# Own places for the queries and keys of heads 2 to 5 in a planned attention and two-layer feed-forward kernel on Trainium2

## The chip, the cores and the metric

The kernel runs on one NeuronCore of one Trainium2 chip. The metric is the device time of one execution in microseconds (us), from the first instruction to the last. The kernel before was timed three times: 1030.91, 1033.85 and 1034.68 us, median 1033.85 us. A core has five engines that run side by side and wait for each other by semaphores: TensorE (PE, with its weight loads in a row of their own, PEld), VectorE (DVE), ScalarE (ACT), GpSimd (POOL) and SyncE (SP). In this kernel SP issues every transfer between main memory and the core, one after the other.

## What is computed

```python
def reference(q, k, v, s, moe_w_a, moe_w_b, moe_w_out, moe2_w_in, moe2_w_out):
    # 4 batches, 8 heads, 576 positions, head size 64; float64 weights, float32 q, k, v, s
    scores = q @ k.T / sqrt(64)
    cum = cumsum(maximum(s, 0))
    scores = where(causal, -1e9, scores + minimum(-(cum[:, None] - cum[None, :]), 0))
    attn = exp(scores - max(scores)); attn /= sum(attn) + 1e-9
    x = (attn @ v) with heads side by side        # 2304 x 512
    x = ((x @ w_a) * (x @ w_b)) @ w_out           # inner width 1536
    r = maximum(x @ w_in, 0); return (r * r) @ w_out2   # inner width 2048
```

## The kernel before, in words

The weights arrive as 64-bit words. "Decoding" turns a block of them into two float32 halves (`wh`, a high part, and `wl`, a low part) with a handful of ACT, DVE and POOL instructions (`split_w`, `decode`, `words`); raw words are fetched into the places `roomxh`, `roomxl` and `words`. Products of the feed-forward layers are three matmuls each (high by high, high by low, low by high).

The first batch's attention is the prologue. `attention(0)` runs over four pairs of heads. For each pair `prep_first` (L531) fetches the values, calls `load_first` (L434) for each head to fetch keys (`fk`) and queries (`fq`) as 64 x 576 tiles, fetches one row of running sums into `fk` as a 65th row, and scales the queries by ACT or DVE (`scaled`). `softmax` then computes scores `st` on PE, row maxima `neg` on DVE and exponentials `e` on ACT; `weigh` transposes (`pt`), copies (`ph`) and multiplies by the values (`av`); `divide` does the division (`rs`). Two banks named `s` hold the first two score pieces of a head, so a head's first piece waits until the exponentials of the head before it have read that bank.

`load_first` takes `fq` from two tiles of the tag `T2q` in turn, and `fk` from the tag `T2k`, which has two buffers. Head 2 therefore waits for head 0, head 3 for head 1, and so on.

The first feed-forward layer of the first 512 positions (`moe1(0)`, "chunk 0", the products `ab` and `py`) follows, with the decoding of its 36 weight blocks and the attention of batch 1 laid between; then come batches 2 and 3, further chunks, and the second layer.

The order of all instructions is made by a planner (`Plan.order`), before anything runs, from costs that are written in the code: each engine takes the operation of lowest rank that can start now by these costs. Where a matmul bank would be taken up after a gap of over 400 ns by the planner's reckoning, the planner puts idle matmuls of the constant tile `warm` before it (`op.idle`), one for each 230 ns of gap; 40 more such matmuls (`glow`, rank `fill`) go wherever PE has nothing else. All of them are called fillers here. They take PE's time and compute nothing.

```python
                gap = t - max(free[e], min(op.bank.tag.free))
                if gap > self.GAP:
                    op.idle = max(op.idle, int(gap / self.BURN))
```

Of the kernel before, what the change touches and what calls it, by code (L numbers as in the profile page):

```python
# [7 lines left out]
F32 = mybir.dt.float32  # L8
# [8 lines left out]
P = 128  # L17
# [246 lines left out]
def attention_moe_moe(tc, q, k, v, s, w_a, w_b, w_out, w_in2, w_out2, out):  # L264
    nc = tc.nc
    B, H, D, S = q.shape
    DM, NT = out.shape
# [9 lines left out]
    GRP = 3  # L277
    GB = 4
# [3 lines left out]
    W = 512  # L282
# [33 lines left out]
    def pool(name):  # L316
        return lambda: pools[name]

    def gated(name, shape, dtype, tag, bufs, nm):
        return pl.tile(pool(name), shape, dtype, tag, bufs, nm, swapped)  # L320

    def sb(shape, dtype, tag, bufs, name):
        return pl.tile(pool("sb"), shape, dtype, tag, bufs, name)

    def at(shape, dtype, tag, bufs, name):
        return gated("at", shape, dtype, tag, bufs, name)
# [38 lines left out]
    def dma(out, in_, kb, takes=(), lag=0.0):  # L365
        pl.call(("SP", kb * 3.0, False, "dma_start", (out, in_), {}), takes=takes, lag=lag)
# [44 lines left out]
    def load_values(b, p):  # L411

        t = at([P, NJ, P], F32, "val", 2, f"val{b}_{p}")
        j = 0
        while j < len(kb):
            k0, m = kb[j]
            j1 = j + 1
            while j1 < len(kb) and kb[j1][1] == m:
                j1 += 1
            dma(  # L420
                t[:m, j:j1].part(j),
                v[b, p, k0 : k0 + m * (j1 - j)].rearrange("(j t) c -> t j c", t=m), m * (j1 - j) * 0.5,
            )
            for i in range(j, j1):
                values[b, p, i] = t[:m, i].part(j)
            j = j1
# [2 lines left out]


    first_q = [at([P, S], F32, "T2q", 2, f"fq{i}") for i in range(2)]
    first_k = {}

    def load_first(hh):  # L434
        tq = first_q[hh % 2]
        tk = first_k[hh] = at([P, S], F32, "T2k", 2, f"fk{hh}")
        dma(tk[:D].part("x"), k[0, hh], S * 0.25)
        dma(tq[:D].part("x"), q[0, hh], S * 0.25)

# [11 lines left out]
    for hh in range(2):  # L451
        load_first(hh)
# [55 lines left out]
    def scaled(n, t):  # L508

        pl.call(  # L510
            on_dve("tensor_scalar", n, t, t, D**-0.5, None, op0=ALU.mult, two=True, each=0.52),
            on_act("mul", n, t, t, D**-0.5),
        )
# [17 lines left out]
    def prep_first(p):  # L531

        load_values(0, p)
        heads = []
        for hh in (2 * p, 2 * p + 1):
            if hh not in first_k:
                load_first(hh)
            tk = first_k[hh]
            dma(tk[D : D + 1].part("c"), cum[hh : hh + 1], 2)
            tq = first_q[hh % 2]  # L540
            scaled(S, tq[:D].part("x"))
            heads.append((tq, tk))
        return heads
# [230 lines left out]
    def attention(b):  # L774
        steps = []

        def unit(p):
            st = {}

            def begin():  # L780
                st["h"] = prep_first(p) if b == 0 else prep(b, p)

            def one(h):
                def f():
                    if h == 0:
                        st["u"] = at([P, S], F32, "u", 2, f"u{b}_{p}")
                        st["one"] = at([P, 2 * len(kb)], F32, "one", 2, f"one{b}_{p}")
                    st[h] = softmax(b, p, h, st["h"][h], st["one"])
                    if h == 1:
                        u = st["u"]  # L790
                        for chunk in weight_banks:
                            weigh(b, p, (st[0], st[1]), chunk, u)
                        divide(b, p, st["one"], u)
                        if b == 0:
                            xh, xl = first_x(p, 0, FIRST)
                            copy(FIRST, xh, u[:, :FIRST])
                            subtract(FIRST, xl, u[:, :FIRST], xh.bitcast(F32))
                            dma(xd[b][0][p].part(p), u[:, FIRST:], (S - FIRST) * 0.5)
                        else:
                            dma(xd[b][0][p].part(p), u, S * 0.5)  # L800

                return f

            steps.extend([begin, one(0), one(1)])
# [789 lines left out]
```

## Time and profile before

| | |
|---|---|
| runs of the kernel before | 1030.91, 1033.85, 1034.68 us |
| profiled execution, span | 1037.2 us (no separate time of this execution is given) |
| PE busy, PEld busy | 1004.5 us (97%), 872.1 us (84%) |
| DVE, ACT, POOL busy | 754.7 (73%), 605.2 (58%), 348.0 us (34%) |
| mean granted TensorE clock | 0.993 of full speed |
| transfers | 243.55 MB, 235 GB/s |

Fillers count as busy PE time. A row of the timeline gives the start, the duration (of several, from the first start to the last end), the engine, the operation with its tiles, and in brackets how long the engine stood idle before it and what ended that. Rows of SPq are issues of transfers; when the data landed is read from the instruction that waited for it.

### The profile page before, as it was taken

To read this page: it belongs to the slowest core of one execution; us is meant where nothing else is said; L and a number is where in the kernel's file an instruction comes from. 1 tells how busy PE (TensorE), PEld (TensorE's weight loads), DVE (VectorE), ACT (ScalarE), POOL (GpSimd) and SP (SyncE) were. 2 spreads that over 40 slices of the span, in tenths; PEclk is the share of its full clock that TensorE was granted. 3 is DMA by queue.
4 is the path that set the end of the run, shared out by engine and by line. 5 is a ranking of instruction groups with operands and counts; after the bars stand their busy time and mean duration, and the time that the engine had idled before them with its cause. 6 is when DMAs were issued, how large, how long until landed. Compare 5 with 4: busy or idle time off the path is not lost.

```text
span 1037.2 us, 16852 instructions
## 1 busy us (share of the span) xinstructions
PE 1004.5 (97%) x5639; PEld 872.1 (84%) x5639; DVE 754.7 (73%) x1557; ACT 605.2 (58%) x1374; POOL 348.0 (34%) x309
## 2 busy tenths in 40 slices
PE   9998989998999999999999999999999999999998
PEld 5667767675778777788889999989999999999998
DVE  5888888767677787346698888688767766876566
ACT  5875768665666665233344454487556665657562
POOL 2233525446444542011122324222325212441123
PEclk9999999999999999999999999999999999999999
DMA  8447687788778786656665767489968866778664
GB/s 218 134 138 217 177 285 209 256 242 259 215 231 239 208 260 210 192 182 228 226 194 177 239 190 262 160 316 366 344 239 330 298 236 253 264 255 296 248 235 162
DMA packets 139254, 243.55 MB, mean 235 GB/s; under 512 B 21272, under 2 KB 91024, under 8 KB 139168
## 3 DMA queue, kind: packets, MB, share of 16 engines
q1 hardware_dynamic: 139168, 242.49, 72.1%
q8 instruction: 44, 0.72, 0.3%
q14 instruction: 42, 0.34, 0.1%
HBM read 181.46 MB, written 52.11 MB: 225 GB/s over the span
## 4 chain that ended last, share of the span: by engine, by line
PE 76%; DMA 12%; DVE 4%; ACT 3%; issue 2%; POOL 1%; SPq 1%; DVEq 0%; POOLq 0%; ACTq 0%
PE ab L261 13%; PE pa L261 9%; PE py L261 8%; PE po_0t L261 6%; PE pw L261 5%; PE pc L261 4%; PE wa L261 4%; PE st L261 4%; PE av L261 3%; PE pt L261 3%; PE wc L261 2%; PE pb L261 2%; PE po_0b L261 2%; PE po_3b L261 2%; PE po_2b L261 2%; PE po_1b L261 2%
## 5 line engine op out<-in xcount | busy, mean ns | idle before, releaser
L261 ACT ACTIVATE e<-st,neg 120x288 f32<-120x288 f32 (+3 forms) x192 | 93.4, 490 | 33.8 <-DVE neg L261 32.1
L261 PE MATMUL py<-g,wh 128*128 128x512 f32 x288 | 93.4, 406 | 1.9 <-DVE y L261 1.5
L261 PE MATMUL ab<-xh,wh 128*128 128x512 f32 x192 | 77.3, 402 | 0.0
L261 PE MATMUL ab<-xh,lo 128*128 128x512 f32 x192 | 75.6, 394 | 0.0
L261 PE MATMUL ab<-xl,wh 128*128 128x512 f32 x192 | 75.5, 393 | 0.0
L261 PE MATMUL pt<-ident,e 120*120 120x120 f32 (+2 forms) x480 | 69.6, 272 | 6.1 <-ACT ph L261 4.8
L261 PEld LDWEIGHTS pt<-ident,e 120*120 120x120 f32 (+2 forms) x480 | 50.5, 134 | 26.9 <-issue 10.1
L261 PEld LDWEIGHTS py<-g,wh 128*128 128x128 f32 x288 | 53.7, 193 | 12.9 <-DVE y L261 1.8
L261 DVE CUSTOM_DVE_ANT_0 st<-st,mask 120x336 f32<-120x336 f32 (+4 forms) x120 | 52.9, 456 | 13.7 <-PE st L261 12.3
L261 PE MATMUL ab<-x,wh 128*128 128x512 f32 x192 | 62.1, 405 | 0.0
L261 PE MATMUL av<-ph,val 120*64 120x240 f32 (+3 forms) x512 | 58.7, 360 | 0.0
L261 PE MATMUL py<-g,loo 128*128 128x512 f32 x144 | 57.5, 399 | 0.0
L261 DVE COPY ph<-pt 120x360 f32<-120x360 f32 (+3 forms) x82 | 42.1, 529 | 17.5 <-PE pt L261 16.3
L261 PE MATMUL st<-T 66*120 66x336 f32 (+1 forms) x144 | 44.8, 324 | 8.9 <-ACT e L261 7.6
L261 PEld LDWEIGHTS av<-ph,val 120*64 120x64 f32 (+1 forms) x512 | 31.3, 136 | 22.6 <-issue 10.5
L261 ACT COPY ph<-pt 120x360 f32<-120x360 f32 (+3 forms) x78 | 34.0, 446 | 18.0 <-PE pt L261 17.4
L261 DVE TENSOR_TENSOR ab<-ab,a 128x512 f32<-128x512 f32 x36 | 25.2, 699 | 24.8 <-PE ab L261 23.3
L261 PEld LDWEIGHTS ab<-xh,lo 128*128 128x128 f32 x192 | 36.5, 190 | 8.0
L261 PEld LDWEIGHTS ab<-xh,wh 128*128 128x128 f32 x192 | 36.4, 190 | 7.1
L261 PEld LDWEIGHTS ab<-xl,wh 128*128 128x128 f32 x192 | 36.5, 190 | 6.9
L261 ACT CAST g<-ab 128x512 fp32r<-128x512 f32 x36 | 21.1, 585 | 35.8 <-DVE ab L261 35.7
L261 PEld LDWEIGHTS ab<-x,wh 128*128 128x128 f32 x192 | 35.5, 191 | 7.5
(693 smaller groups left out, 3166.6 us busy)
## 6 DMA issues: line engine op xcount, KB each, us to landing
w<-w2q SPq DMA_DIRECT2D x48, 896.0 KB
lo<-wlab SPq DMA_DIRECT2D x36, 512.0 KB
w2q<-w2ip SPq DMA_DIRECT2D x48, 256.0 KB
w2s<-w2op SPq DMA_DIRECT2D x48, 256.0 KB
loo<-wlo SPq DMA_DIRECT2D x24, 384.0 KB
w2ir<-in_moe_w_in SPq DMA_DIRECT2D x16, 512.0 KB
w2or<-in_moe_w_out SPq DMA_DIRECT2D x16, 512.0 KB
ws_0t<-w2s SPq DMA_DIRECT2D x12, 512.0 KB
```

Of the source, the lines that this page charges most:

```text
L261: getattr(eng, method)(*map(real, args), **{k: real(a) for k, a in kw.items()})
```

## The change

Head 2 and 3 get tiles of the tag `g` (four buffers), heads 4 and 5 tiles of `loo` for the queries and `lo` for the keys; these tags serve the feed-forward layers later. Heads 6 and 7 take the two old query tiles again. Every query tile gets its row of ones from POOL at the start, six where there were two. Nothing else is edited.

```diff
     first_q = [at([P, S], F32, "T2q", 2, f"fq{i}") for i in range(2)]
+    first_q += [sb([P, 2 * W], F32, "g", GB, f"fq{i}")[:, :S] for i in (2, 3)]
+    first_q += [sb([P, 2 * GRP * P], F32, "loo", 2, f"fq{i}")[:, :S] for i in (4, 5)]
+    AHEAD_HEADS = len(first_q)
     first_k = {}
 
     def load_first(hh):
-        tq = first_q[hh % 2]
-        tk = first_k[hh] = at([P, S], F32, "T2k", 2, f"fk{hh}")
+        tq = first_q[hh % AHEAD_HEADS]
+        if hh in (2, 3):
+            tk = sb([P, 2 * W], F32, "g", GB, f"fk{hh}")[:, :S]
+        elif hh in (4, 5):
+            tk = sb([P, 2 * DM], F32, "lo", 3, f"fk{hh}")[:, :S]
+        else:
+            tk = at([P, S], F32, "T2k", 2, f"fk{hh}")
+        first_k[hh] = tk
         dma(tk[:D].part("x"), k[0, hh], S * 0.25)
         dma(tq[:D].part("x"), q[0, hh], S * 0.25)
@@ prep_first
-            tq = first_q[hh % 2]
+            tq = first_q[hh % AHEAD_HEADS]
```

Since a planner sets the order, the edit moves instructions on all engines. Three places follow.

SP, the transfers after the first values, before: `fk_213` is head 2's key, `roomxh`, `roomxl` and `words` take the first weights.

```order
L261 DMA val_1_120<-in_v 120x4x128
L261 DMA cd<-cl 32x576
L261 DMA roomxh<-in_moe_w_a 128x4x256
L261 DMA roomxh<-in_moe_w_b 128x4x256
L261 DMA roomxl<-in_moe_w_out 128x1024
L261 DMA words_199<-in_moe_w_a 128x4x256
L261 DMA fk_213<-in_k 64x576
L261 DMA fq_87<-in_q 64x576
```

And in the changed program (`fk_143`, `fq_131` are head 2's, `fk_164`, `fq_141` head 3's).

```order
L261 DMA val_1_120<-in_v 120x4x128
L261 DMA fk_143<-in_k 64x576
L261 DMA fq_131<-in_q 64x576
L261 DMA fk_143<-cum 1x16x36
L261 DMA fk_164<-in_k 64x576
L261 DMA fq_141<-in_q 64x576
L261 DMA fk_164<-cum 1x16x36
L261 DMA fk_176<-in_k 64x576
```

Nine more transfers follow before the first weights do: the rest of heads 4 and 5 with the second half of `cd` among them, and head 6's three, which wait for head 0's tiles. The first weight transfer stands 15 places later than before.

ACT, from the scaling of head 0's queries to head 0's exponentials, before:

```order
L261 ACTIVATE fq_87<-fq_87 64x576
L261 CAST ch<-cum 32x576
L261 ACTIVATE fq_102<-fq_102 64x576
L261 ACTIVATE e_0_0_188,sum_133<-st_0_0_0_155,neg_131 120x336
L261 ACTIVATE e_0_0_188,sum_133<-st_0_0_0_155,neg_131 96x96
```

And changed:

```order
L261 ACTIVATE fq_87<-fq_87 64x576
L261 CAST ch<-cum 32x576
L261 ACTIVATE fq_102<-fq_102 64x576
L261 ACTIVATE fq_131<-fq_131 64x576
L261 ACTIVATE fq_141<-fq_141 64x576
L261 ACTIVATE e_0_0_208,sum_192<-st_0_0_0_145,neg_188 120x336
L261 ACTIVATE e_0_0_208,sum_192<-st_0_0_0_145,neg_188 96x96
```

The scaling of heads 2 and 3 now stands ahead of head 0's first exponential. Heads 4 to 7 are scaled by DVE.

PE, from head 0's last score piece to head 1's first, before:

```order
L261 MATMUL st_0_0_3_196<-fk_79,fq_87 120x456
L261 LDWEIGHTS plain
L261 MATMUL st_0_0_3_196<-mask,plain 120x120
L261 MATMUL st_0_1_0_204<-fk_93,fq_102 120x336
L261 LDWEIGHTS plain
L261 MATMUL st_0_1_0_204<-mask,plain 120x120
```

And changed:

```order
L261 MATMUL st_0_0_3_170<-fk_79,fq_87 120x456
L261 LDWEIGHTS plain
L261 MATMUL st_0_0_3_170<-mask,plain 120x120
L261 LDWEIGHTS warm
L261 MATMUL glow<-warm 128x512
```

The last two rows stand there eleven times, and head 1's first piece follows them. Counted over the whole program, PE has 5248 matmuls of the computation in both, and 87 fillers before, 97 after. Before, 13 fillers stand between head 1's pieces and head 2's first piece, with 13 transposes (`pt`) of heads 0 and 1 among them; after, 11 stand before head 1, 1 within it and 7 before head 2, and the 13 transposes come later. From there to the first product of chunk 0 there are 21 before and 20 after. In chunk 0 there are none before, and 9 and 2 after (at a `pt` of batch 1's first pair and at a `py` of the second group). Up to the start of chunk 2 the change has 6 fewer (5 at a `py`, 1 at chunk 2's first product). From chunk 2 on no filler is left, and the two programs run almost in the same order.

## Rows read from the trace of the kernel before

**Rows 1.** The page, busy time by engine (microseconds, share of the span, instructions).

```profile
PE 1004.5 (97%) x5639; PEld 872.1 (84%) x5639; DVE 754.7 (73%) x1557; ACT 605.2 (58%) x1374; POOL 348.0 (34%) x309
```

**Rows 2.** Windows: stretch, length, busy time by engine, granted clock, DMA share, GB/s.

```profile
20.00:40.00 20.00, 18.93 (x125) 12.57 (x123) 15.32 (x44) 14.66 (x39) 7.63 (x6) 1.00 0.65 176
40.00:60.00 20.00, 20.00 (x151) 14.10 (x149) 16.03 (x46) 15.04 (x49) 5.12 (x4) 1.00 0.38 113
60.00:80.00 20.00, 19.39 (x126) 11.99 (x124) 16.81 (x36) 14.88 (x35) 6.42 (x5) 1.00 0.51 152
...
500.00:1040.00 540.00, 524.24 (x2950) 507.38 (x2948) 397.81 (x695) 300.29 (x602) 159.63 (x140) 1.00 0.72 252
```

**Rows 3.** Timeline of PE, from head 1's first score piece to head 2's.

```profile
13.04 0.78 PE L261 MATMUL st<-fk,fq 65*120 65x336 f32 x2
...
16.62 0.81 PE L261 MATMUL glow<-warm 128*128 128x512 bf16 x3
...
17.27 0.76 PE L261 MATMUL pt<-ident,e 96*96 96x96 f32 x6
...
17.87 1.03 PE L261 MATMUL glow<-warm 128*128 128x512 bf16 x4
...
18.87 1.07 PE L261 MATMUL pt<-ident,e 120*120 120x120 f32 x7
...
19.78 1.46 PE L256 MATMUL st<-warm 128*128 128x512 bf16 x6
...
22.22 0.83 PE L261 MATMUL st<-fk,fq 65*120 65x336 f32 x2 [0.98 <-DVE fq L261]
```

**Rows 4.** Timeline of SP's issues and of what waited for queries, first 22 us.

```profile
3.07 0.60 SPq L261 DMA_DIRECT2D fq<-in_q  x1
...
6.25 0.69 ACT L261 ACTIVATE fq<-fq 64x576 f32<-64x576 f32 x1 [0.21 <-DMA fq<-in_q]
...
7.82 0.44 SPq L261 DMA_DIRECT2D cd<-cl  x1
...
8.30 0.42 SPq L261 DMA_DIRECT2D roomxh<-in_moe_w_a  x1
...
13.73 0.60 SPq L261 DMA_DIRECT2D fq<-in_q  x1
...
14.37 0.59 SPq L261 DMA_DIRECT2D fk<-cum  x1
15.01 0.58 SPq L261 DMA_DIRECT2D words<-in_moe_w_b  x1
...
21.71 0.45 DVE L261 TENSOR_SCALAR fq<-fq 64x576 f32<-64x576 f32 x1 [2.46 <-DMA fq<-in_q]
```

**Rows 5.** Timeline of ACT and DVE, head 0's maxima and exponentials.

```profile
10.88 0.67 DVE L261 TENSOR_REDUCE neg<-st 120x1 f32<-120x336 f32 x2 [4.06 <-PE st L261]
...
11.67 0.54 ACT L261 ACTIVATE e<-st,neg 120x336 f32<-120x336 f32 x1 [4.74 <-DVE neg L261]
...
12.66 0.44 ACT L261 ACTIVATE e<-st,neg 120x216 f32<-120x216 f32 x1
```

**Rows 6.** Timeline of PE, its stalls of over 1 us in chunk 0.

```profile
103.41 0.47 PE L261 MATMUL st<-T 66*120 66x456 f32 x1 [2.02 <-ACT e L261]
...
141.39 0.39 PE L261 MATMUL st<-T 66*120 66x288 f32 x1 [2.68 <-ACT e L261]
...
187.22 0.98 PE L261 MATMUL pt<-ident,e 120*120 120x120 f32 x4 [1.45 <-ACT ph L261]
```

**Rows 7.** Windows of 4 us around the second of these, columns as in rows 2.

```profile
140.00:144.00 4.00, 2.61 (x10) 2.21 (x11) 3.59 (x9) 2.88 (x9) 0.95 (x1) 0.87 0.67 173
144.00:148.00 4.00, 4.00 (x17) 3.20 (x17) 1.81 (x4) 1.37 (x4) 0.00 (x0) 0.70 1.00 341
```

**Rows 8.** Timeline, chunk 0's first product and the start of the stages after it.

```profile
76.14 0.58 PE L261 MATMUL ab<-x,wh 128*128 128x512 f32 x1
...
85.63 0.57 ACT L261 CAST g<-ab 128x512 fp32r<-128x512 f32 x1
...
90.11 0.55 SPq L261 DMA_DIRECT2D loo<-wlo  x1
```

## The prediction, made before the changed kernel ran

> **What bounds the kernel now.** I read the page first, then windows over the whole span, then the timeline of PE with its stalls, then the timelines of SP and ACT in the first 25 us. The page [rows 1] says that PE is busy 97% of the span, and the windows [rows 2] say the same of nearly every stretch: the first batch's attention has a full 20.00 us between 40 and 60 us, 18.93 between 20 and 40, and 19.39 between 60 and 80. Part of this is filler, so the timeline has to be looked at as well [rows 3]. Head 1's scores start at 13.04 us and are done at 16.62; head 2's start at 22.22. Between them lie 13 transposes and 13 fillers, and a stall of 0.98 us that the scaling of head 2's queries ended. Why that scaling is late, SP and DVE show [rows 4]: the queries were asked for at 13.73 us, behind four weight transfers, and DVE could start on them at 21.71, 7.98 us later. Queries asked for at 3.07 us, with little else in flight, were in use at 6.25, after 3.18 us. So the change goes at a real wait. The question is what it is worth once the fillers and the order of the other engines have moved too.
>
> Behind the prologue the stalls of PE are few: in chunk 0 there are three of 2.02, 2.68 and 1.45 us, all ended by ACT [rows 6]. After the second the granted clock is 0.87 and 0.70 in two stretches of 4 us [rows 7], a mix of PE's two levels, 2.4 and 1.2 GHz; that is 4 x 0.13 + 4 x 0.30 = 1.7 us on top of the stall.
>
> **The prologue, step by step.** Head 0's scores end at 13.04 us in both programs, for all that stands ahead of them on SP is the same, and the four extra memsets on POOL come after the two that head 0 needs; the memsets that they delay (of the maxima's tiles) would be in use at 10.88 us [rows 5], long after.
>
> *PE.* A filler costs (17.27 - 16.62) / 3 = 0.217 us [rows 3]. Now 11 of them come first, 2.39 us. Head 1's pieces, with the three transposes among them, take 16.62 - 13.04 = 3.58 us as before; one filler among them and seven behind are 1.74 us. Head 2 then starts at 13.04 + 2.39 + 3.58 + 1.74 = 20.75 us, 1.47 us sooner. But the 13 transposes that stood before it are still to do, and cost 17.87 - 17.27 = 0.60 and 19.78 - 18.87 = 0.91, or 1.51 us [rows 3]. With them PE is at 22.26 us where it was at 22.22: **0.0 us**. The wait of 0.98 us goes, and six more fillers, 1.30 us, take its place.
>
> *ACT.* The scaling of heads 2 and 3 now stands ahead of head 0's first exponential, which started at 11.67 us [rows 5]. SP issued `cd` at 7.82 us, where head 2's key will now be, and issues one transfer each 0.64 us (13.73, 14.37, 15.01) [rows 4]. Head 3's queries are four places behind: 7.82 + 4 x 0.64 = 10.38 us. With the 3.18 us of the quiet row they land at 13.56; after the scaling of 0.69 us [rows 4] the first exponential starts at 14.25, 2.6 us late. Behind it on ACT is all of head 0; who waits is PE, for the bank of head 1's first piece. That bank is free 12.66 - 11.67 = 0.99 us after the first exponential starts [rows 5], at 15.24. PE's eleven fillers end at 13.04 + 2.39 = 15.43. So the delay is just covered, with 0.2 us to spare, and I cost it at nothing. At the far end, with the 7.98 us of the loaded row, the queries land at 18.36, and PE waits 4.6 us. I take the quiet row, since the weights that shared the queue in the other now come after; the traffic is only the heads' own.
>
> The Trainium skill speaks against the change at this place: "TensorE: Matmul & The Clock Gate", Part 2, on each phase, says that PE is the only engine that reorders, so exponentials that could run stand still behind a scaling that waits for its data. By that rule the late landing gives the slower rival below; were ACT free to pass, there would be no such case. No row here shows it either way.
>
> *The rest of the prologue.* From 22 to 76 us PE has one filler less, -0.2 us, and otherwise the same matmuls; the stalls that are left there are 0.61 us between 60 and 80 us [rows 2]. The gain here can't be above about 0.8 us: the fillers are in the program and PE has to run them.
>
> *The weights.* Their first transfer stands 15 places later, 8.30 + 15 x 0.64 = 17.9 us [rows 4]. The first product starts at 76.14 us [rows 8], which covers it; what is lost is the head start for the blocks after. At that product the changed program has decoded 5 high parts where it had 8, and fetched 11 blocks where it had 12; at the second group of `py` it is level again (22 to 20 high parts). Cost 0 if ACT and DVE catch up in their idle time, else the slower rival. The other moved transfer, `cd`, is read in batch 1 alone, after 76 us.
>
> *The borrowed tiles.* Head 5's scores are done by 60 us, the first new use of `g` is at 85.63 us and of `loo` at 90.11 [rows 8]. So nothing waits for them: 0.
>
> **Chunk 0 and after.** There the changed program has 11 fillers that were not there, 11 x 0.217 = +2.4 us, and up to chunk 2 six fewer, -1.3 us. Both are bounded by zero: where PE would stall anyway, a filler costs nothing, and where a stall is left bare, a missing filler saves nothing. I count both in full: +1.1 us, between -1.3 and +2.4. From chunk 2 on the order is nearly the same, and PE is busy 524.24 of the 537 us that are left from 500 us on [rows 2]; 0.
>
> **Sum.** 0.0 - 0.2 + 1.1 = **+0.9 us**, with bounds of -2.3 and +2.4 before the rivals. The profiled execution spans 1037.2 us, so it would become 1038.1; that execution is 3.35 us above the median of the three runs, 1033.85, and the same sum on the median is **1034.8 us**. A measurement can tell about 0.5% from no change, 5.2 us.
>
> **The rivals.** *Slower, head 3's queries land late.* One place: ACT's fifth ACTIVATE. If the queries take longer than 3.18 + 0.2 us, PE waits for each further microsecond. At the loaded row's 7.98 us it is 4.6 us, and a clock that falls as at 141 us adds 1.7: +6.3, or 1041 us. For: three transfers of values and one of sums are still in flight just before. Against: no weights are. Chance 0.12.
>
> *Slower, the decoding stays behind.* Three high parts less at 76 us mean that ACT, which ended all three stalls of chunk 0, has more to do in it. Two further stalls like the one at 141 us with their clock, 2 x (2.68 + 1.7) = 8.8, of which the 11 fillers cover 2.4: +0.9 + 6.4, or 1041 us. It decides from the point where a product of chunk 0's third or fourth step waits for `wh`. Chance 0.16.
>
> *Faster, stalls of chunk 0 go.* The new order shifts ACT's work against PE's there. If the stalls at 141 and 187 us vanish with their clock, that is 2.68 + 1.45 + 2 x 1.7 = 7.5 us: 1034.8 - 7.5 = 1027 us. For: all the stalls hang on ACT's order, which is new. Against: nothing in the change relieves ACT. Chance 0.17.
>
> *Faster, PE is not the bound of the prologue.* If matmuls and fillers only looked busy, DVE with 15.32 and 16.03 us in the 40 us from 20 to 60 [rows 2] would set the pace, and earlier queries could take up to 40 - 31.35 = 8.7 us off: 1026 us. Against it stands that the matmuls there follow each other without a stall. The Trainium skill's "Perfetto Trace Analysis", Identifying the Most-Contended Engine, holds for it: matmul busy time is a poor measure and weight loads are the better one; by the loads, 12.57 and 14.10 us, PE had room. Chance 0.05.
>
> *The fetches don't come early.* The order shows that they do, so only 0.02, and the time is then as before.
>
> **How the numbers follow.** The forecast has 0.48; its own range is 1031 to 1038, the bounds with the spread of the runs. With the rival that changes nothing, "same" is 0.50. Faster is 0.17 + 0.05 = 0.22, slower 0.12 + 0.16 = 0.28. The range takes in the slower rivals at 1041 and the larger faster one at 1027, and reaches from 1026 to 1042 us; what it leaves out is stalls in greater number on either side.
>
> **What would show it.** Right: head 0's first exponential near 14.2 us with DMA as its releaser, head 2's first piece near 20.8 with no wait for `fq`, the first `ab` within 1 us of 76.14. Wrong: PE waiting between the eleven fillers and head 1; stalls in chunk 0 ended by `wh` or by a weight transfer; the first `ab` more than 2 us earlier; or a difference that first arises after 400 us.

## The result, and the profile after

The changed kernel took 1042.2 us (median of 12 runs, 1039.33 to 1050.82), the kernel before 1034.09 us (12 runs, 1030.53 to 1039.33): a ratio of 1.0087, 95% interval 1.0065 to 1.0109. It is slower by 0.9%, or 8.1 us, where the forecast was no change.

The page's busy times and three windows answer to [rows 1, 2].

```profile
PE 1008.8 (97%) x5640; PEld 873.3 (84%) x5649; DVE 752.0 (72%) x1559; ACT 610.1 (58%) x1385; POOL 329.4 (32%) x300
```

```profile
20.00:40.00 20.00, 19.55 (x142) 13.65 (x142) 15.44 (x45) 14.02 (x46) 3.79 (x3) 1.00 0.73 225
...
60.00:80.00 20.00, 19.82 (x128) 13.25 (x127) 16.05 (x37) 14.75 (x35) 5.07 (x4) 1.00 0.62 179
...
500.00:1040.00 540.00, 527.37 (x2949) 508.18 (x2947) 399.08 (x695) 302.67 (x607) 153.84 (x141) 1.00 0.72 250
```

PE is as busy as before, and even in the prologue a little busier. The prologue itself answers to [rows 3 to 5]. The timelines of SP, ACT and PE in it, and of chunk 0's first product [rows 8]:

```profile
10.24 0.59 SPq L261 DMA_DIRECT2D fq<-in_q  x1
...
17.75 0.58 SPq L261 DMA_DIRECT2D roomxh<-in_moe_w_a  x1
...
13.29 0.68 ACT L261 ACTIVATE fq<-fq 64x576 f32<-64x576 f32 x1 [0.54 <-DMA fq<-in_q]
13.88 0.52 ACT L261 ACTIVATE e<-st,neg 120x336 f32<-120x336 f32 x1
...
12.92 2.54 PE L261 MATMUL glow<-warm 128*128 128x512 bf16 x10
15.29 0.73 PE L261 MATMUL st<-fk,fq 65*120 65x336 f32 x2
...
20.55 0.73 PE L261 MATMUL st<-fk,fq 65*120 65x336 f32 x2
...
74.77 0.81 PE L261 MATMUL ab<-x,wh 128*128 128x512 f32 x2
```

Head 3's queries, asked for at 10.24 us, let the first exponential start at 13.88; head 1 follows the fillers at 15.29 without a wait, head 2 starts at 20.55 (22.22 before) and chunk 0 at 74.77 (76.14 before). The weights are first asked for at 17.75 us, 9.45 us later than before. Of chunk 0, [rows 6] is not the whole: in the kernel before it lasts until chunk 1's first product at 258.80 us, and three more stalls of PE in it are over 1 us, one of 1.26 us at 180.64 us, ended by ACT, and two ended by a transfer:

```profile
235.19 0.38 PE L261 MATMUL st<-T 66*120 66x336 f32 x1 [1.24 <-DMA t2k<-kh]
...
236.92 0.38 PE L261 MATMUL st<-t2k,t2q 128*120 128x336 f32 x1 [1.34 <-DMA t2k<-kh]
```

The three longest after, up to chunk 1's first product at 257.36 us, were all ended by ACT. The longest two are 1.84 us each, in place of 2.68 and 2.02:

```profile
116.97 0.40 PE L261 MATMUL st<-T 66*120 66x288 f32 x1 [1.30 <-ACT e L261]
...
138.69 0.47 PE L261 MATMUL st<-T 66*120 66x456 f32 x1 [1.84 <-ACT e L261]
...
255.37 0.54 PE L261 MATMUL st<-T 66*120 66x216 f32 x1 [1.84 <-ACT e L261]
```

Up to chunk 2 these two executions show no loss. Chunk 2's first product, before and after:

```profile
433.83 0.58 PE L261 MATMUL ab<-xh,wh 128*128 128x512 f32 x1
```

```profile
433.60 0.58 PE L261 MATMUL ab<-xh,wh 128*128 128x512 f32 x1
```

At 533 us they are still level. There the last group of chunk 2's `py` runs beside the first products of the stage that takes the remaining 768 positions in two halves of 384 (tiles `wa`, `wb`, `wc`, `pw`; called the wide stage below). PE before:

```profile
533.09 0.73 PE L261 MATMUL py<-g,wh 128*128 128x512 f32 x2 [1.47 <-DVE y L261]
...
542.56 0.33 PE L261 MATMUL wb<-b21hx,wh 128*128 128x384 f32 x1
...
667.60 0.33 PE L261 MATMUL pa<-b11h,w 128*128 128x384 f32 x1
```

and after:

```profile
533.07 0.73 PE L261 MATMUL py<-g,wh 128*128 128x512 f32 x2 [0.70 <-DVE y L261]
...
545.10 0.44 PE L261 MATMUL wb<-b21hx,wh 128*128 128x384 f32 x1 [2.40 <-DVE y L261]
...
672.56 0.34 PE L261 MATMUL pa<-b11h,w 128*128 128x384 f32 x1
```

From level at 533 us the changed kernel falls 4.96 us behind by the second layer's first product (`pa`). 2.40 us of that is one stall, which the addition `y` on DVE ended. DVE and the transfer it waits for, before:

```profile
536.85 0.55 SPq L261 DMA_DIRECT2D lo<-wlab  x1
...
538.72 1.22 DVE L261 TENSOR_TENSOR wx<-ws,wx 128x1024 fp32r<-128x1024 f32 x1
539.87 0.68 DVE L261 TENSOR_TENSOR y<-py,y 128x512 f32<-128x512 f32 x1
...
543.59 1.28 DVE L261 TENSOR_TENSOR ws<-wh,lo 128x512 f32<-128x512 f32 x2
544.79 0.68 DVE L261 TENSOR_TENSOR y<-py,y 128x512 f32<-128x512 f32 x1
```

and after:

```profile
536.77 0.55 SPq L261 DMA_DIRECT2D lo<-wlab  x1
...
538.71 1.23 DVE L261 TENSOR_TENSOR wx<-ws,wx 128x1024 fp32r<-128x1024 f32 x1
542.23 2.21 DVE L261 TENSOR_TENSOR ws<-wh,lo 128x512 f32<-128x512 f32 x2 [2.30 <-DMA lo<-wlab]
544.37 1.28 DVE L261 TENSOR_TENSOR y<-py,y 128x512 f32<-128x512 f32 x2
```

DVE is free at the same moment in both, and `lo` was asked for at the same moment. Before, DVE adds the first `y` ahead of the sums `ws`, and when it comes to these at 543.59 us, nothing has to be waited for. After, both `ws` stand ahead of both `y`: DVE waits 2.30 us for `lo`, `y` waits behind, and with `y` the bank that `wb` needs. Then the granted clock falls. The windows from 540 us, before and after (columns as in [rows 2], the clock third from the end):

```profile
540.00:544.00 4.00, 4.00 (x22) 3.63 (x21) 3.97 (x6) 0.89 (x2) 1.40 (x1) 1.00 0.91 323
544.00:548.00 4.00, 4.00 (x23) 3.78 (x23) 3.79 (x9) 0.79 (x2) 0.00 (x0) 1.00 0.84 271
```

```profile
540.00:544.00 4.00, 2.70 (x14) 2.10 (x12) 1.77 (x2) 0.61 (x2) 3.29 (x3) 1.00 1.01 309
544.00:548.00 4.00, 2.90 (x10) 2.90 (x11) 3.28 (x8) 0.69 (x1) 0.00 (x0) 0.69 0.85 292
548.00:552.00 4.00, 4.00 (x20) 3.61 (x19) 1.80 (x6) 1.03 (x2) 0.00 (x0) 0.88 0.69 205
```

At 0.69 and 0.88 of 2.4 GHz, a mix with 1.2 GHz, 4 x 0.31 + 4 x 0.12 = 1.7 us go. With the stall that is 4.1 of the 4.96 us; for the rest no single row was found. Another 1.5 us are lost between there and the end (spans 1037.2 and 1043.7 us), which is no more than profiled executions differ by: over the 18 of this case that last stretch takes 366.6 to 373.1 us. No instruction named here reads the first batch's queries.

### The profile page after: what moved, and what is told of

Its sections match the earlier page's. It is cut to its first block, busy times and chain, and to the rows that moved or that the text cites. A ratio compares the mean times of both kernels' runs of the same rounds, so it can differ in the third digit from the quotient of the medians.

```text
span 1043.7 us, 16850 instructions
## 1 busy us (share of the span) xinstructions
PE 1008.8 (97%) x5640; PEld 873.3 (84%) x5649; DVE 752.0 (72%) x1559; ACT 610.1 (58%) x1385; POOL 329.4 (32%) x300
## 4 chain that ended last, share of the span: by engine, by line
PE 59%; DMA 4%; DVE 3%; ACT 1%; issue 1%; SPq 0%; DVEq 0%; POOL 0%; ACTq 0%
PE ab L261 9%; PE pa L261 8%; PE po_0t L261 6%; PE py L261 5%; PE pw L261 4%; PE pc L261 4%; PE wa L261 4%; PE wc L261 2%; PE pb L261 2%; PE po_3b L261 2%; PE po_1b L261 2%; PE po_0b L261 2%; PE po_2b L261 2%; PE po_3t L261 1%; PE po_1t L261 1%; PE av L261 1%
## 5 line engine op out<-in xcount | busy, mean ns | idle before, releaser
L261 PE MATMUL py<-g,wh 128*128 128x512 f32 x288 | 90.8, 396 | 1.3 <-DVE y L261 0.7
L261 ACT COPY ph<-pt 120x360 f32<-120x360 f32 (+3 forms) x87 | 38.2, 450 | 30.7 <-PE pt L261 29.9
L261 DVE COPY ph<-pt 120x360 f32<-120x360 f32 (+3 forms) x73 | 37.6, 524 | 12.1 <-PE pt L261 11.8
L261 PE MATMUL st<-t2k,t2q 128*120 128x336 f32 (+1 forms) x144 | 40.2, 303 | 0.4 <-DMA t2k<-T 0.2
```

The lines of the kernel that those rows point to most:

```text
L261: getattr(eng, method)(*map(real, args), **{k: real(a) for k, a in kw.items()})
```

## The experiments

Each ratio is to the kernel before on the same chip, with its 95% interval. The kernel before measured 1033.5 to 1034.87 us beside them.

**Head or tail: e1 and e2.** The order up to chunk 2's first product comes from one kernel, the rest from the other.

```diff
+OWN, TAIL, CUT = True, False, (2, 0, 0)   # e1; e2: False, True
...
+        at = next(i for i, op in enumerate(mine) if op.key == self.cut)
+        head, rest = mine[:at], {op.key: op for op in mine[at:]}
+        for key, eng, idle in tail:
+            if key in rest:
+                op = rest.pop(key)
+                op.eng, op.idle = eng, idle
+                head.append(op)
+        return head
```

> The changed kernel up to the first product of chunk 2; from there on the order of the kernel before. Theory A (the loss is made by the new order of the last chunk before the second layer, where DVE's wait for `lo` stands ahead of the additions `y`): the changed prologue and chunks 0 and 1 cost nothing (in the two traces chunk 2's first product starts at 433.8 and 433.6 us), so the ratio to the kernel before is 1.000, between 0.997 and 1.003, and the 2.40 us stall of PE behind `y` is gone. Theory B (the loss belongs to the early fetch and its new tiles, wherever it shows): the ratio stays at 1.009, above 1.005.

> The mirror: the kernel before with its own tiles and order up to the first product of chunk 2, from there on the order that the changed kernel has. Theory A: the loss is here, a ratio of 1.005 to 1.009, with a PE stall of about 2.4 us before the second `wb` of the last chunk and a clock window of about 0.8 behind it. Theory B: no loss, 0.997 to 1.003.

Measured: e1 1037.65 us, 1.0027 [1.0007, 1.0047]; e2 1041.13 us, 1.0048 [1.0025, 1.0072]. Both ends cost, the tail too, which the edit does not touch; the two intervals overlap, so which costs more does not follow from these. e2 has the stall before `wb` (2.23 us), e1 has not.

**The two additions: e3 and e4.** The changed kernel with `ws` moved behind `y` on DVE, and the kernel before with `ws` moved ahead.

```diff
+    ws = [order[place["ws", i]] for i in range(2)]
+    if MOVE == "y first":        # e3
+        to = max(place["y", 2], place["y", 3])
+        keep = [op for op in order if op not in ws]
+        n = keep.index(order[to]) + 1
+    else:                        # e4
+        n = min(place["y", 2], place["y", 3])
+        keep = [op for op in order if op not in ws]
+        n = keep.index(order[n])
+    order = keep[:n] + ws + keep[n:]
```

> The changed kernel, with one move on DVE: the two additions `ws` of the last chunk's fourth block, which wait for `lo`, stand behind the two additions `y` instead of ahead of them. Theory A: the 2.40 us stall and the clock loss of 1.7 us behind it go, so the time falls by about 4 us, to a ratio of about 1.005 to the kernel before; the rest of the loss, which arises later in the same chunk, stays. Rival (the stall only moves to the next wait on DVE): under 1.5 us better, a ratio above 1.007.

> The kernel before, with the opposite move: the two additions `ws` stand ahead of the two additions `y`. Theory A: DVE waits for `lo` until about 542 us, PE stalls some 2.4 us behind it and loses 1.7 us of clock, so the ratio is about 1.003 to 1.004. Rival (in the old order `lo` has landed in time, or the stall is caught up later): within 1.001.

Measured: e3 1038.26 us, 1.0029 [1.0012, 1.0046]; e4 1039.99 us, 1.0052 [1.0033, 1.007]. Two instructions of DVE take 0.58% off the changed kernel (1.0087 to 1.0029), and the same two put 0.52% on the kernel before. In e3 DVE's `y` waits only for PE, `ws` for nothing, and `wb` starts without a stall:

```profile
541.25 0.69 DVE L281 TENSOR_TENSOR y<-py,y 128x512 f32<-128x512 f32 x1 [1.14 <-PE py L281]
541.86 2.18 DVE L281 TENSOR_TENSOR ws<-wh,lo 128x512 f32<-128x512 f32 x2
...
542.12 0.33 PE L281 MATMUL wb<-b21hx,wh 128*128 128x384 f32 x1
```

In e4 the wait and the stall are there, in a kernel that is otherwise the one before:

```profile
538.03 1.29 DVE L281 TENSOR_TENSOR ws<-wh,lo 128x512 f32<-128x512 f32 x2 [2.28 <-DMA lo<-wlab]
...
539.98 0.44 PE L281 MATMUL wb<-b21hx,wh 128*128 128x384 f32 x1 [1.47 <-DVE y L281]
```

Two things say that these two additions are all of the tail's loss that can be told from the noise. e3, with the new tail and `y` first, measured the same as e1 with the old tail (1.0029 and 1.0027). And from chunk 2's first product to the first `pa`, the four profiled executions with `ws` ahead of `y` and a stall at `wb` (after, e2, e4, n2) take 238.96, 236.90, 238.65 and 238.51 us, the other 14 all 233.5 to 234.3.

**Chunk 0's fillers: e5.** e1 without the 9 and 2 fillers of chunk 0.

```diff
+    for op in order:
+        if op.key < pl.cut if op.key is not None else False:
+            op.idle = 0 if op.idle in (2, 9) else op.idle
```

> The kernel of the first experiment (changed kernel up to chunk 2, old order from there, ratio 1.0027) without the 9 and 2 fillers that the changed order has in chunk 0. Theory A (these fillers are the rest of the loss): 11 x 0.217 = 2.4 us come back, a ratio of 1.000 to 1.001, with PE going on to the same products without a stall. Rival (PE waits there anyway, for ACT or DVE, and loses clock on top): the ratio stays at 1.002 to 1.005.

Measured: 1039.08 us, 1.0049 [1.0025, 1.0073], not below e1. The fillers are not what the head loses by. In the stretch from 125 to 150 us PE is busy 19.41 us, in e1 22.72: idle time has taken their place.

**The tiles without the order: e6 and e7.** e6 has the new tiles, and on every engine, SP's fetches among them, the order of the kernel before. e7 is e6 without the 13 fillers ahead of head 2.

```diff
+        for key, eng, idle in tail:
+            op = rest.pop(key)
+            op.eng, op.idle = eng, idle
+            head.append(op)
...
+    glows = [op for op in order if op.rank[0] == 4][18:25]   # e7
+    order = [op for op in order if op not in glows]
+    [op for op in order if op.idle][2].idle = 0
```

> One part of the change alone: heads 2 to 5 have their own tiles, but every engine keeps the order of the kernel before. SP no longer waits for head 0's tiles, so head 2's fetch goes out right behind the fourth weight transfer, near 10.4 instead of 13.2 us, and lands behind 2 MB of weights. Theory A (what costs is the new order, not the tiles): the 0.98 us stall before head 2 shrinks or goes, nothing else changes, a ratio of 0.998 to 1.001. Rival (tiles in other places or earlier traffic cost by themselves): above 1.002.

> The last one, and the 13 fillers between head 1's scores and head 2's are left out, 2.8 us of PE. If the fillers held PE back once the queries are early, head 2 starts up to 2.8 us sooner than there and chunk 0's first product with it: a ratio of 0.996 to 0.999. If PE waits for the fetch, the exponentials or the copies there anyway, the idle time takes their place: 0.999 to 1.002, or more where the granted clock falls behind the idle time.

Measured: e6 1034.84 us, 1.0000 [0.9977, 1.0023]; e7 1035.55 us, 1.0013 [0.9988, 1.0039]. The tiles cost nothing. Of e7 the section on the hardware says more.

**The same without the edit: n2.** The kernel before with one constant of the planner changed by one, and nothing else. **n2y** is n2 with `ws` moved as in e3.

```diff
-    LATE = {"PE": 120.0, "DVE": 90.0, "ACT": 120.0, "POOL": 120.0, "SP": 2000.0, "CTL": 0.0}
+    LATE = {"PE": 120.0, "DVE": 90.0, "ACT": 121.0, "POOL": 120.0, "SP": 2000.0, "CTL": 0.0}
```

> The kernel before with one number of the planner changed, ACT's delay of 120.0 ns to 121.0, an edit that does nothing on the chip but gives another order. Theory C (the size of the loss is that of any new order, not of the early fetch): the time moves by 0.3 to 1% too, most likely up. Rival (a new order alone costs nothing, the loss needs the early fetch): within 0.2% of the kernel before.

> The kernel before with one planner constant changed by one (ACT's delay 121 for 120, no tile and no fetch changed), which alone took 1042.95 us, and with the two ws additions put behind the two y additions on DVE. If the place of these two additions is the greater part of what a re-planned order costs here too, 1036 to 1039 us, without the stall of 2.2 us before the wide stage's third wb product and without the half clock behind it. If the re-planned order loses elsewhere, 1042 to 1043 us still.

Measured: n2 1042.95 us, 1.0082 [1.0045, 1.0119]; n2y 1039.52 us, 1.0054 [1.0032, 1.0076]. A re-planned order costs as much as the change did, with no tile and no fetch changed. n2 has the same two rows:

```profile
538.64 2.68 DVE L261 TENSOR_TENSOR ws<-wh,lo 128x512 f32<-128x512 f32 x2 [1.66 <-DMA lo<-wlab]
...
541.98 0.47 PE L261 MATMUL wb<-b21hx,wh 128*128 128x384 f32 x1 [2.23 <-DVE y L261]
```

In n2y they are gone, and `wb` starts at 536.14 us with no stall. Its time is just above what was expected, and the two intervals overlap, so the times alone don't show what the additions cost n2. n2y is clear of the kernel before all the same: something else is left, and no run shows what.

**Where in the head: e8, e9, e11, e12.** As e1, with the cut at chunk 0's first product (e8), chunk 1's (e9), head 2's first score (e11) and head 4's (e12).

```diff
-OWN, TAIL, CUT = True, False, (2, 0, 0)
+OWN, TAIL, CUT = True, False, (0, 0, 0)   # e8; e9: (1, 0, 0)
...
+            if (b, hh, i) == CUT:             # e11: (0, 2, 0); e12: (0, 4, 0)
+                pl.cut = pl.key
             pe(cost, calls, ps, ins)
```

> The changed kernel's order up to chunk 0's first product, and from there the order of the kernel before. The kernel that kept the new order up to chunk 2 lost 0.27% (1037.65 us) and its trace stood some 4 to 5 us behind at batch 1's scores in chunk 0. Theory A, the new order inside chunks 0 and 1 is what costs it: this one is within 0.1% of the kernel before, 1034 to 1035.5 us. Theory B, what the prologue hands over (fewer decoded weights, transposes left for later) costs it: 1037 to 1038 us again, with the delay in the old order's waits at the start of chunk 0.

> The changed kernel's order through chunk 0, the old order from chunk 1's first product on. If chunk 0 (or the prologue) is the place, 1037 to 1038 us as with the cut at chunk 2; if chunk 1 is the place, 1034 to 1035.5 us, as the kernel before.

> The changed kernel's order on every engine up to head 2's first score piece (the eleven fillers, the early scaling and fetches in it), the old order of all that is left from there. If these first 21 us cost it, 1037 to 1040 us as with the whole new prologue; if what follows in the prologue does, 1034 to 1035.5 us.

> The same cut at head 4's first score piece, in the middle of the prologue. Together with the cuts at head 2 and at chunk 0 it brackets the place: 1034 to 1035.5 us if the second half of the new prologue costs the 0.3 to 0.6%, 1037 to 1040 us if the first half does.

Measured: e8 1039.65 us, 1.0050 [1.0025, 1.0075]; e9 1039.97 us, 1.0059 [1.0038, 1.008]; e11 1043.31 us, 1.0095 [1.0071, 1.012]; e12 1046.5 us, 1.0125 [1.0098, 1.0152]. e9 costs no less than e1, so the new order of chunk 1 is not needed for the head's loss. The other three do not place it further, for each stops PE near its own join, where the old order takes over from the new. In e8 that is at the start of chunk 0, where ACT waits for a weight:

```profile
87.21 0.67 ACT L280 ACTIVATE roomxl<-roomxl 128x512 f32<-128x512 f32 x1 [2.53 <-DMA roomxl<-in_moe_w_out]
...
90.82 1.22 PE L280 MATMUL ab<-x,wh 128*128 128x512 f32 x2 [3.63 <-DVE g L280]
```

Between 74 and 100 us the changed kernel, e1, e3, e5 and e9 have no stall above 0.2 us. e11 stops for 3.65 us at 24.23 us and e12 for 3.80 at 39.84, both behind a copy `ph` on DVE. So e8 does not show that the prologue's new order costs anything where chunk 0's new order follows it.

**The edit without the planner: e10.** Own tiles, and on SP alone the new order up to chunk 0. The other engines keep theirs.

```diff
+NEW = ('SP',)
...
+        order = {}
+        for e in self.LATE:
+            order[e] = [x for x in (by_new if e in NEW else by_old) if x[1] == e]
```

> The own tiles and, on SP alone, the changed kernel's order up to chunk 0: the queries and keys of heads 2 to 5 are asked for early and the first weights 15 places later, while PE, ACT, DVE and POOL keep every instruction, filler and place of the kernel before. This is the edit without what the planner made of it. If the fetch is a gain by itself, the stall of 1 us before head 2 goes and the time is 1033 to 1034 us. If the late weights are what the new prologue costs (its order alone measured 1037.65 to 1039.97 us in four kernels), 1038 to 1040 us, with waits for wh or for a weight transfer in the prologue or chunk 0. If it is the order of the other engines' work, within 0.15% of the kernel before.

Measured: 1048.46 us, 1.0155 [1.0127, 1.0183], the slowest of all, and beyond each of the three expectations. The timelines of DVE and PE, and the window, show why:

```profile
21.76 0.43 DVE L328 TENSOR_SCALAR roomxh<-roomxh 128x512 f32<-128x512 f32 x1 [6.51 <-DMA roomxh<-in_moe_w_a]
...
23.66 1.23 PE L328 MATMUL pt<-ident,e 120*96 120x120 f32 x5 [6.20 <-ACT e L328]
...
20.00:40.00 20.00, 16.34 (x104) 11.03 (x105) 13.75 (x40) 12.40 (x35) 5.09 (x4) 0.83 0.55 171
```

The first decoding step stands on DVE amid the row maxima of head 1. It waits 6.51 us for weights that were asked for at 17.76 us; behind it wait the maxima, the exponentials and PE, and the clock of 0.83 costs another 20 x 0.17 = 3.4 us. Together 9.6 us, of which 6.5 are left at chunk 0's first product (82.67 us, 76.14 before); by chunk 2's it is 9.6 again (443.42 and 433.83).

**The edit with the weights in place: e13 and e14.** The old order on every engine, own tiles. e13 pulls the transfers of heads 2 to 5 forward only behind the first four weights; e14 pulls head 2's alone ahead of them.

```diff
+EARLY, ANCHOR = (2, 3, 4, 5), 2   # e13; e14: (2,), "cl"
...
+        keys = [k for hh in EARLY for k in self.marks[hh]]
...
+        early = [by[k] for k in keys]
...
+        head = keep[:at] + early + keep[at:]
```

> The old order on every engine, own tiles, and on SP the transfers of heads 2 to 5 pulled forward only to the place that head 2's have in the kernel before, behind the first four weights. Theory, the lateness of the first weights is the whole price of the early fetch in e10 (1048.46 us, with DVE standing 6.5 us at a decoding step): with those weights in place it is gone, 1033.5 to 1036 us. Rival, the early fetch costs by its traffic or by the places that it takes on SP from the weights behind: 1038 us or more, with waits for words or for raw queries.

> The old order on every engine, own tiles, and only head 2's three transfers ahead of the first weights, which come 3 x 0.64 = 1.9 us later. In e10 the first weight landed 4.0 us after its issue; here that is at about 8.3 + 1.9 + 4.0 = 14.2 us, and the decoding step on DVE starts at 15.5, so it should not wait. Head 2's queries are there early, and a stall of up to 1 us before head 2 goes: 1033 to 1035 us. If weights later by 2 us cost already, 1037 us or more.

Measured: e13 1036.32 us, 1.0022 [1.0003, 1.0042]; e14 1034.46 us, 1.0003 [0.9982, 1.0025]. With the weights in place nearly all of e10's loss is gone. e10 has other transfers of SP in new places too, but with the 6.51 us in its trace the weights' lateness is its main cause. In e14 the decoding step runs when DVE reaches it:

```profile
15.61 0.41 DVE L292 TENSOR_SCALAR roomxh<-roomxh 128x512 f32<-128x512 f32 x1
```

e14 has head 2's queries early and no wait for them, and gains nothing that its interval could show. In e13 all twelve transfers share the stretch behind the weights, and head 2's queries are as late as in [rows 4]:

```profile
21.90 0.45 DVE L292 TENSOR_SCALAR fq<-fq 64x576 f32<-64x576 f32 x1 [3.09 <-DMA fq<-in_q]
```

No version was faster than the kernel before.

## Why the prediction was wrong, point by point

**What bounds the kernel: right, but only for the stretch that was read.** The wait for head 2's queries was real in that execution, but it is not there each time: e2 and e4 have the prologue of the kernel before, and in their profiled executions head 2 starts at 21.47 and 21.35 us without a wait, with the queries as late as before. In e2:

```profile
20.27 0.45 DVE L280 TENSOR_SCALAR fq<-fq 64x576 f32<-64x576 f32 x1 [0.62 <-DMA fq<-in_q]
...
21.47 0.73 PE L280 MATMUL st<-fk,fq 65*120 65x336 f32 x2
```

The fillers ahead of head 2 cover it there. e14, with the queries early, starts head 2 at 21.45 and stays at 1.0003 [0.9982, 1.0025]; a gain of 0.98 us, 0.1%, would be too small for these runs to tell.

**The prologue: right.** The first exponential was put at 14.25 us and came at 13.88, with a DMA as the releaser of the scaling ahead of it; head 1 at 15.43 and 15.29; head 2 at 20.75 and 20.55; chunk 0's start within 1 us of 76.14, and it was 74.77, 1.4 us earlier; most of that is the stall of the one execution, for e2 and e4 start chunk 0 at 75.28 and 75.16. The quiet row was the right choice for the landing. The borrowed tiles at 0 were right (e6, 1.0000).

**Chunk 0's fillers, +1.1 us: not borne out.** e5 has eleven fillers fewer than e1 and is not faster. By its trace they stood in time that PE would have idled away, which the step had as its bound of zero.

**"From chunk 2 on the order is nearly the same ...; 0": this is the step that failed.** It took nearly the same for the same. Two additions out of some 1,500 instructions on DVE had moved ahead of a third, the first `y`, and in e3 and e4 that is worth 0.58% and 0.52%, or 5 to 6 us: the stall, and in most of the traces the clock behind it. The text even named "a difference that first arises after 400 us" among what would show it wrong, but gave it no price and no chance. The order could have been read there: an instruction that waits for a transfer had come to stand ahead of one that PE waits for. The Trainium skill's "TensorE: Matmul & The Clock Gate", Part 2, on each phase, which the prediction used for ACT, says that only PE reorders; it holds for DVE in this trace, where `y` stands behind `ws` for the 2.30 us. It was applied to the one engine and place that the edit touched.

**The weights, "Cost 0 if ACT and DVE catch up", and the rest of the head: 0.3 to 0.6% in place of nothing.** e1, e5 and e9, all with the new order through chunk 0 and the old tail, measured 1.0027, 1.0049 and 1.0059. The rival "the decoding stays behind" had about this price in total (1041 us) but another place: no stall of over 1 us in chunk 0 was ended by `wh`; that the measured 1042.2 us lies next to it is luck. What is shown: the loss comes with the new order of prologue and chunk 0 (e9), not with the tiles (e6) nor with chunk 0's fillers (e5); the early fetch by itself costs 1.55% through late weights (e10), and 0.2% or nothing where the weights stay in place (e13, e14). That the planner, which moved the decoding back to suit late weights, turned those 1.55% into 0.3 to 0.6% is a reading that fits these and is not shown; which wait carries it in the changed kernel is open. The two profiled executions could not show it, since they are level at 433 us. The one of before was a late one there: of four executions with the old prologue (before, e2, e4, e6) chunk 2's first product starts at 433.83, 429.70, 429.77 and 430.97 us, mean 431.1; of six with the new (after, e1, e3, e5, e8, e9) at 433.60, 435.16, 434.16, 435.73, 431.27 and 435.24, mean 434.2. That is 3.1 us, or 0.3%, between means whose ranges overlap. The planner's other order, n2 and n2y, is not late there (431.33 and 428.10), so not every new order brings this loss.

**The sum.** Instead of +0.9 us: some 3 from the head (e1, e3 and the 3.1 us above) and 5 to 6 from the wide stage, against 8.1 measured.

**The other rivals.** Head 3's queries landed in time (13.29 us). The prediction's three stalls of chunk 0, "all ended by ACT", were six over 1 us, two of them ended by a transfer. The longest became shorter (1.84 us in place of 2.68), and it did not show: chunk 0 takes 182.7 us to chunk 1's first product before and 182.6 after. That PE is not the bound of the prologue found no support: with the queries early, no part of the 8.7 us came off that shows (e14).

## What to carry to other kernels

Where a planner sets the order, an edit's smallest part may be the edit: n2, with one cost changed by one, lost about as much as this change. So the difference of the two orders is to be read to the end on every engine, above all for an instruction that waits for a transfer and has moved ahead of one on which PE depends; and the edit is tested by holding the order fixed (e6, e14), or a re-planned order is taken for the cause. A fetch that is pulled forward delays those it passes: ask what stands behind the first use of each.

## What the runs showed of the hardware that was not expected

A short stall can cost twice, but need not. The 2.40 us before `wb` were followed by 1.7 us of lower clock, while the kernel before passes the same place at 1.00. n2's 2.23 us came with 0.78 and 0.79 in the two windows from 540 us. In e2 the same stall, as long as in n2 and ending at 540.74 us, left the clock at 1.00:

```profile
540.00:544.00 4.00, 3.26 (x18) 3.13 (x19) 3.91 (x10) 0.69 (x1) 0.00 (x0) 1.00 0.82 283
544.00:548.00 4.00, 4.00 (x22) 3.60 (x21) 1.52 (x4) 1.70 (x4) 0.00 (x0) 1.00 0.58 177
```

From chunk 2 to the first `pa` e2 takes 236.90 us, the three whose clock fell 238.5 to 239.0: by these, an estimate, some 2 us are the clock's. What decides which of the two comes, no run shows.

Fillers ahead of head 2 were worth their time in one execution. In the profiled one of e7, which has 13 fewer, PE's granted clock stood at 0.50, that is 1.2 GHz, from 20 to 32 us:

```profile
20.00:24.00 4.00, 2.46 (x8) 1.52 (x10) 2.26 (x6) 1.61 (x3) 1.78 (x2) 0.50 1.07 250
24.00:28.00 4.00, 4.00 (x20) 2.77 (x17) 1.42 (x4) 2.08 (x6) 0.63 (x1) 0.50 0.85 269
```

Chunk 0 started at 80.54 us there and at 75.18 in e6, 5.4 us later for 2.8 us of fillers saved (13 x 0.217). Over twelve runs the two kernels can't be told apart (1035.55 and 1034.84 us).
